# Products of r and v placed in the bank of the product of a, with three operand buffers and two of `ad`

## The chip, the cores and the metric

The kernel runs on one core of one Trainium2 chip. The metric is the device time of one execution in microseconds (us): the kernel before takes 1320.08 us in the median of 3 runs (1316.49 to 1322.68).

A core has five engines that run side by side, each through a list of instructions in a fixed order: TensorE (PE, matrix products, with its weight loads as PEld), VectorE (DVE), ScalarE (ACT), GpSimd (POOL) and SyncE (SP). SP does no arithmetic here; it issues the transfers between memory and the chip (DMAs), one after the other. An instruction whose input isn't ready holds up all that stand behind it on its engine.

## The reference

The input goes through three layers. The first is a recurrence over 768 time steps, for each of 4 x 8 heads with a state of 40 x 40:

```
for t in range(S):
    y[t]  = r[t] @ state
    Sa    = state @ a[t]
    state = state * w[t] - outer(Sa, b[t])
    state = state + outer(v[t], k[t])
```

The other two are gated layers on 3072 tokens of 320 values: `(sigmoid(x @ w_gate) * (x @ w_val)) @ w_out` with 1536 hidden columns, then `h = x @ w_in; (h * sigmoid(1.702 h)) @ w_out` with 2048. The output has 3072 x 320 values.

## The kernel before

**The recurrence in chunks.** The 768 steps are cut into 24 chunks of 32, and each chunk into two halves of two batches each; half h = 0 to 47 belongs to chunk h // 2. Within a chunk the steps are joined to matrix products, and a triangular system takes the place of the step by step update. For a half there are:

- the front (`fronts`, DVE with some help of POOL): running products of w (L699, L705), then `ad` (L728, L740: a scaled, and the decays) and `kb` (L742, L718: b and k scaled). `ad` has four buffers for the first four halves and one for all others.
- the scores (`back`): 16 small products of `ad` and `kb` on PE into the bank pair `s`; DVE multiplies them by masks into `nl` (L795, the triangular system) and `kl` (L802), ACT copies the rest into `kl` (L804). SP stores `nl` as `ldr` (L827), and `ad` and `kl` as `ad_d` and `kl_d` (L809, L812), from where they come back as `ad_l` and `kl_l` when their half's turn comes (L904, L906), some 8 halves later.
- the solve (`solve`): the system of one chunk, or of two after the first four, is loaded (L847), solved by 31 pairs of a multiply and an add (L857, L860), on DVE for the first three chunks and on POOL for the others, stored (L864) and loaded again as `tn` (L874).
- r and v (`preps`, `later`): SP loads r, vt and vn into one of two sets of buffers; PE multiplies r by v (L919) into the same bank pair `s`, and DVE masks that into `vu` (L921).
- the chain (`chain`), which carries the state: PE multiplies `vu` by `kl`, and r by the state `sd`; ACT copies to `xh` (L973); PE multiplies `xh` by a (the "product of a"); ACT copies to `rs` (L1003); PE multiplies `rs` by `tn`, the solved system; DVE's masked copy puts the result into `vu` (L1017); PE multiplies `vu` by `kl` into `po`, from where the next state (L1030, L1037) and the output `yt` (L1052) come.

From half 4 on there is one bank pair `s` for the scores, for r and v, and for the chain's products; the other is given to the first gated layer.

**The gated layers** (`moe1`, `moe2`). The first layer works on pairs of chunks as their outputs come in. Its products (`gv`, `xa`) fill PE between those of the recurrence. The second (`ph`, `y`) begins when the first is done; its weights are decoded on DVE, ACT and POOL once the recurrence has ended.

**The order of the work.** All of this is written as threads, which ask for an engine with a cost, for a buffer (`Slots`) or for an event. A planner (class `Plan`) plays them through, takes for each engine the thread with the lowest key among those that can begin, and writes the instructions in that order. The chip then follows these lists; it doesn't reorder for lateness.

Of the kernel before, what the change touches and what calls it, by code (L numbers as in the profile page):

```python
# [34 lines left out]
C_ID, C_I2, C_UM, C_VM, C_UP, C_SEL, C_END = 0, 128, 168, 200, 234, 306, 338  # L35
# [28 lines left out]
def layout(inp):  # L64
# [13 lines left out]
    def times_on_rows(x):  # L78

        y = x.reshape(2, 2, 2, 2, 2, NCH, C, D)  # L80
        y = np.stack([y[:, :, :, 0], y[:, :, :, 1, ::-1]], axis=3)
        return np.ascontiguousarray(y.transpose(5, 0, 4, 6, 3, 1, 2, 7)).reshape(2 * NCH, 2, C, 8, D)
# [148 lines left out]
def program(ctx: ExitStack, tc: tile.TileContext, abkw, rt, vt, vn, cst, x2, x4, in_r, in_k, in_v, in_w, in_a, in_b, moe_w_gate,  # L231
# [19 lines left out]
    umask, vmask, upred = k[:, C_UM : C_UM + C], k[:, C_VM : C_VM + LT], k[:, C_UP : C_UP + C + D].bitcast(I32)  # L251
# [342 lines left out]
    ring = 2  # L594
# [9 lines left out]
    ads = [wpool.tile([R, I0 + D], F32, tag=f"X{8 + i}", name="ad0") for i in range(4)] + [at.tile([R, I0 + D], F32, name="ad")]  # L604
# [7 lines left out]
    def dims(j):  # L612
        return slice(J * j, J * j + D)
# [7 lines left out]
    def turn_of(h):  # L621

        return h if h < 4 else h % 2
# [29 lines left out]
    e_b, e_vu, e_y = ([Event() for _ in range(NH)] for _ in range(3))  # L653
# [26 lines left out]
    def fronts():  # L680

        thread = plan.current
        for h in range(NH):
# [42 lines left out]
            ad = ads[min(h, START)]  # L726
# [38 lines left out]
    def back(h, kb, ad):  # L765
# [14 lines left out]
        if q == 0:  # L780
            yield nl_slots
            nls[c] = at.tile([128, 2, 8, C], F32, tag="nl", name="nl", bufs=2)
        i = place_of(h)
        yield "PE", 0.55, None, None, plan.WAITS, s_slots[i]
# [7 lines left out]
        if q == 1:  # L792
            yield e_lower_first[c]
# [3 lines left out]
        if q == 0:  # L797
            plan.set(e_lower_first[c])
        else:
            plan.start(scores_out(c), f_key(h) - 0.3, plan.done + plan.LATENCY)  # L800
        yield "DVE", 0.38
        nc.vector.tensor_mul(klv[:, :, :, 0:LT], pt[:, :, :, 0:LT], vmask.unsqueeze(1).unsqueeze(1).broadcast_to([128, 2, 4, LT]))  # L802
# [4 lines left out]
        if h >= START:  # L807
            yield "SP", 0.5
            nc.sync.dma_start(out=st["ad_d"], in_=ad[:, A0:I0])  # L809
            plan.give(ad_slots)  # L810
            yield "SP", 0.5, -9.0
            nc.sync.dma_start(out=st["kl_d"], in_=kl)  # L812
            plan.give(kl_slots)
        plan.set(e_stored[h])

    nls, ldrs = {}, {}
    e_lower_first = [Event() for _ in range(NCH)]

    def scores_out(c):
        cs = group_of[c]  # L820
        if cs not in ldrs:
            ldrs[cs] = drp.tile([2, 2, 8 * len(cs), C, C], F32, tag="ldr", name="ldr", bufs=2)
        yield "SP", 1.2
        nl, u0 = nls.pop(c), 8 * (c - cs[0])
        for i in range(2):
            for o in range(2):
                nc.sync.dma_start(out=ldrs[cs][o, i, u0 : u0 + 8].rearrange("u s t -> s u t"), in_=nl[64 * i : 64 * i + C, o])  # L827
        plan.give(nl_slots)
        if c == cs[-1]:
            plan.start(solve(cs, ldrs.pop(cs), nc.vector if c < DS else nc.gpsimd), s_key(cs), plan.done)  # L830

# [48 lines left out]
    def preps():  # L880

        thread = plan.current
        for h in range(NH):
# [6 lines left out]
            if h >= START:  # L890
                yield e_stored[h]
            yield "SP", 2.5
# [3 lines left out]
            for i in range(2):  # L896
                nc.sync.dma_start(out=vu[64 * i + C : 64 * i + 2 * C, :, C:], in_=vn[h, i])
            t_rv = plan.done
            st = half[h]
            st["vu"] = vu  # L900
            if h >= START:
                yield "SP", 1.0, -9.0
                kl = at.tile([128, KL], F32, tag="kl_l", name="kl_l", bufs=2)
                nc.sync.dma_start(out=kl, in_=st["kl_d"])  # L904
                ad = at.tile([R, I0], F32, tag="ad_l", name="ad_l", bufs=2)
                nc.sync.dma_start(out=ad, in_=st["ad_d"])  # L906
                views(h, ad, kl)
                plan.set(e_stored[h], 0.5)
            plan.set(e_b[h])
            plan.start(later(h, r72, vt_, vu), h - 10, t_rv)  # L910
            yield e_vu[h]

    def later(h, r72, vt_, vu):
        i = place_of(h)
        yield "PE", 0.45, None, None, 0, s_slots[i]
        pv = ss[i][:, :, 0 : 4 * C].rearrange("p o (g n) -> p o g n", g=4)
# [3 lines left out]
        yield "DVE", 0.36  # L920
        nc.vector.tensor_mul(vu[:, :, 0:C].rearrange("p (o g) n -> p o g n", o=2), pv,  # L921
                             vmask[:, 0:C].unsqueeze(1).unsqueeze(1).broadcast_to([128, 2, 4, C]))
# [30 lines left out]
    def chain(hb):  # L953
        thread = plan.current
        for h in range(hb, NH, 2):
# [40 lines left out]
            for gi, g2, o, j, x in HEADS:  # L996
                mm(pr[some(j), o, g2], an[dims(j), gi, 0:LT], xh[o][dims(j), g2], False, True)
# [553 lines left out]
```

## Time and profile before

| | |
|---|---|
| median of 3 runs | 1320.08 us |
| profiled execution | 1315.36 us, span 1313.5 us |
| mean clock of TensorE granted | 0.929 of full |
| PE busy | 1141.2 us (87%) |
| DVE, ACT, POOL busy | 774.8, 451.5, 386.6 us |

The span is the time from the first to the last instruction. Busy time says how much an engine had to do; what decides is where it waited and for whom. The list of waits names the waiting line, the line that released it, the total, the number of times and the longest. PEclk is the share of TensorE's full clock of 2.4 GHz that was granted; it has two levels, full and half. Line numbers L... are those of the kernel before; L578 is the helper that issues all matrix products.

### The profile page before, as it was taken

The page shows a single profiled execution, that of the slowest core. Times are in us where ns is not written, and L with a number is a line of the kernel's source. Part 1 is how long each engine was busy: PE and PEld are TensorE (multiplying, and loading weights), DVE is VectorE, ACT ScalarE, POOL GpSimd, SP SyncE. Part 2 cuts the span into 40 slices and gives each one's busy share as a digit, 9 for nine tenths or more (in the row PEclk, how much of TensorE's full clock was granted, in tenths as well). Part 3 has the DMA queues.
Part 4 walks back from the last instruction along what each step waited for, and adds up shares of the span by engine and source line. Part 5 has one row for each costly group of instructions (what it writes and reads, how often), then busy time and mean ns, then how long its engine had stood idle before and what let it go on. Part 6 is the DMA issues. An engine that isn't in the chain of part 4 may idle for free. (4 is left out here: it accounts for less than half of the span.)

```text
span 1313.5 us, 41904 instructions
## 1 busy us (share of the span) xinstructions
PE 1141.2 (87%) x17601; PEld 1041.9 (79%) x17601; DVE 774.8 (59%) x2074; ACT 451.5 (34%) x1114; POOL 386.6 (29%) x840
## 2 busy tenths in 40 slices
PE   2375648889899999979997999999999899999996
PEld 2265547779798898978887989999889798899995
DVE  7977875445454455545463543337999766556552
ACT  1232322223333232323332323336676243434332
POOL 3212753343435352607070615102432000000000
PEclk9965768679999999989998999999999999999998
DMA  6568565656565657465654555424443432322110
GB/s 176 143 172 235 140 187 143 169 147 168 141 171 123 180 124 192 105 165 142 157 158 110 157 126 130 101 59 137 141 122 94 119 107 56 89 59 79 44 43 23
DMA packets 238340, 168.69 MB, mean 128 GB/s; under 512 B 156800, under 2 KB 204480, under 8 KB 238144
## 3 DMA queue, kind: packets, MB, share of 16 engines
q1 hardware_dynamic: 238144, 165.94, 48.1%
q8 instruction: 140, 2.29, 0.7%
q14 instruction: 56, 0.46, 0.1%
HBM read 123.10 MB, written 42.78 MB: 126 GB/s over the span
## 5 line engine op out<-in xcount | busy, mean ns | idle before, releaser
L578 PE MATMUL gv<-xs,w1i 128*128 128x256 f32 x1728 | 270.3, 298 | 3.1 <-ACT xs L439 3.1
L578 PEld LDWEIGHTS gv<-xs,w1i 128*128 128x128 f32 x1728 | 233.4, 199 | 15.7 <-ACT xs L439 3.5
L857 POOL TENSOR_TENSOR ut<-x,u 128x126 f32<-128x126 f32 (+27 forms) x341 | 139.6, 410 | 186.8 <-DMA x<-in_x_dram 154.2
L578 PE MATMUL y<-w2o,g 128*128 128x320 f32 x1152 | 186.0, 310 | 3.8 <-DVE g L1309 3.3
L578 PE MATMUL xa<-g,w1o 128*128 128x256 f32 x1152 | 186.0, 298 | 3.0 <-DVE g L530 1.4
L578 PEld LDWEIGHTS y<-w2o,g 128*128 128x128 f32 x1152 | 177.2, 189 | 12.4 <-DVE g L1309 3.8
L578 PE MATMUL ph<-xs,w2i 128*128 128x512 f32 x672 | 171.2, 394 | 1.9 <-DVE gg L1301 1.8
L578 PEld LDWEIGHTS xa<-g,w1o 128*128 128x128 f32 x1152 | 156.9, 198 | 13.3 <-DVE g L530 2.3
L860 POOL TENSOR_TENSOR x<-x,ut 128x126 f32<-128x126 f32 (+27 forms) x341 | 143.0, 419 | 26.4
L578 PEld LDWEIGHTS ph<-xs,w2i 128*128 128x128 f32 x672 | 122.5, 188 | 24.5 <-DVE gg L1301 3.3
L523 DVE TENSOR_TENSOR sg<-gv,sg 128x256 f32<-128x256 f32 x144 | 60.4, 419 | 126.2 <-ACT sg L521 126.0
L578 PE MATMUL s<-r,vt 40*64 40x32 f32 x1536 | 64.3, 240 | 66.2 <-DVE vu L1017 55.5
L578 PEld LDWEIGHTS s<-r,vt 40*64 40x64 f32 x1536 | 59.0, 158 | 74.8 <-DVE vu L1017 61.6
L521 ACT ACTIVATE sg<-gv 128x256 f32<-128x256 f32 x144 | 55.2, 383 | 178.5 <-PE gv L578 177.1
L528 ACT CAST g<-sg 128x256 fp32r<-128x256 f32 x144 | 58.6, 407 | 130.0 <-DVE sg L523 114.9
L1301 DVE TENSOR_TENSOR gg<-ph,sg 128x512 f32<-128x512 f32 x96 | 66.0, 687 | 49.6 <-ACT sg L1297 49.6
L1307 ACT CAST g<-gg 128x512 fp32r<-128x512 f32 x96 | 59.5, 620 | 94.8 <-DVE gg L1301 94.6
L1309 DVE TENSOR_TENSOR g<-gg,g 128x512 fp32r<-128x512 f32 x96 | 67.2, 700 | 40.4 <-ACT g L1307 40.4
L728 DVE TENSOR_TENSOR ad<-wx,iw 112x256 f32<-112x256 f32 x45 | 24.3, 540 | 111.0 <-DMA ad_d<-ad 110.9
L578 PE MATMUL s<-ad,kb 40*64 40x80 f32 x1536 | 47.8, 273 | 47.6 <-DVE kb L742 15.9
L1297 ACT ACTIVATE sg<-ph 128x512 f32<-128x512 f32 x96 | 57.2, 596 | 87.9 <-PE ph L578 87.8
L530 DVE TENSOR_TENSOR g<-sg,g 128x256 fp32r<-128x256 f32 x144 | 64.0, 444 | 38.9 <-ACT g L528 38.7
(125 smaller groups left out, 1764.8 us busy)
## 6 DMA issues: line engine op xcount, KB each, us to landing
ab<-in_abkw_dram SPq DMA_DIRECT2D x44, 451.9 KB
kl_d<-kl SPq DMA_DIRECT2D x44, 296.0 KB
kl_l<-kl_d SPq DMA_DIRECT2D x44, 296.0 KB
ad_d<-ad SPq DMA_DIRECT2D x44, 252.0 KB
ad_l<-ad_d SPq DMA_DIRECT2D x44, 252.0 KB
r<-in_rt_dram SPq DMA_DIRECT2D x48, 112.0 KB
vt<-in_vt_dram SPq DMA_DIRECT2D x48, 112.0 KB
u<-ldr SPq DMA_DIRECT2D x20, 256.0 KB
```

The source lines that it names most:

```text
L521: nc.scalar.activation(gg, gv[:, 0, :], AF.Sigmoid)
L523: nc.vector.tensor_mul(gg, gv[:, 1, :], gg)
L528: nc.scalar.copy(out=g4[:, 0], in_=gg)
L530: nc.vector.tensor_sub(out=g4[:, 1], in0=gg, in1=g4[:, 0].bitcast(F32))
L578: nc.tensor.matmul(o, lhsT=w, rhs=x, start=start, stop=stop, skip_group_check=True)
L728: either[on].tensor_mul(dd, wx[:, :, 0:C], iw.broadcast_to([R, 8, C]))
L857: eng.tensor_mul(tv, x[:, :n, s : s + 1].broadcast_to([128, n, m]), u[:, s, s + 1 :].unsqueeze(1).broadcast_to([128, n, m]))
L860: eng.tensor_add(x[:, :n, s + 1 :], x[:, :n, s + 1 :], tv)
L1297: nc.scalar.activation(sg, ph, AF.Sigmoid, scale=1.702)
L1301: nc.vector.tensor_mul(gg, ph, sg)
L1307: nc.scalar.copy(out=g4[:, 0], in_=gg)
L1309: nc.vector.tensor_sub(out=g4[:, 1], in0=gg, in1=g4[:, 0].bitcast(F32))
```

## The change

Each half's product of r and v moves: it is now issued by the chain of the half before, right behind the product of a, into columns 384 to 511 of the same banks, which the chain doesn't use (`r_by_v`, `beside`). Its mask (`masked`) follows the chain's masked copy. r, vt and vu have three sets of buffers instead of two. `ad` has two buffers instead of one. The loads of `kl_l` and `ad_l` (K and B) get a thread of their own (`backs`). `nl` is no longer made: the mask for `kl` keeps both parts, and `ldr` is stored out of `kl`, by half instead of by chunk. v's rows come padded with zeros, in one transfer per half instead of two. The planner books 1.5 us more for the stores of `ad` and `kl`.

```diff
--- before.py
+++ after.py
@@ times_on_rows, the layout of v @@
-        return np.ascontiguousarray(y.transpose(5, 0, 4, 6, 3, 1, 2, 7)).reshape(2 * NCH, 2, C, 8, D)
...
+        z = np.zeros((2 * NCH, 2, 2, C, 8 * D), np.float32)
+        z[:, :, 1] = y.reshape(2 * NCH, 2, C, 8 * D)
+        return z.reshape(2 * NCH, 128, 8, D)
@@ program @@
-    umask, vmask, upred = k[:, C_UM : C_UM + C], k[:, C_VM : C_VM + LT], k[:, C_UP : C_UP + C + D].bitcast(I32)
+    umask, vmask, upred = k[:, C_UM : C_UM + LT], k[:, C_VM : C_VM + C], k[:, C_UP : C_UP + C + D].bitcast(I32)
-    ring = 2
+    ring = 3
-    ads = [wpool.tile([R, I0 + D], F32, tag=f"X{8 + i}", name="ad0") for i in range(4)] + [at.tile([R, I0 + D], F32, name="ad")]
+    ads = [wpool.tile([R, I0 + D], F32, tag=f"X{8 + i}", name="ad0") for i in range(4)] + [at.tile([R, I0 + D], F32, name=f"ad_{i}") for i in range(2)]
-        return h if h < 4 else h % 2
+        return (h if h < 2 else h + 1) if h < 4 else (h - 2) % 3
-    wc_slots, ab_slots, suf_slots, wx_slots, kb_slots, ad_slots, kl_slots = Slots(DEPTH), Slots(2), Slots(1), Slots(1), Slots(2), Slots(1), Slots(1)
+    wc_slots, ab_slots, suf_slots, wx_slots, kb_slots, ad_slots, kl_slots = Slots(DEPTH), Slots(2), Slots(1), Slots(1), Slots(2), Slots(2), Slots(1)
-    nl_slots, u_slots, tn_slots, b_slots, po_slots = Slots(2), Slots(2), Slots(2), Slots(0), Slots(1)
+    u_slots, tn_slots, b_slots, k_slots, po_slots = Slots(2), Slots(2), Slots(0), Slots(2), Slots(1)
-            ad = ads[min(h, START)]
+            ad = ads[h if h < START else START + h % 2]
@@ back @@
-        yield "PE", 0.55, None, None, plan.WAITS, s_slots[i]
+        yield "PE", 0.55, None, None, plan.WAITS if h >= 2 * START else 0, s_slots[i]
...
-        yield "DVE", 0.36, plan.LATENCY
-        nc.vector.tensor_mul(nls[c][:, :, 4 * q : 4 * q + 4], pt[:, :, :, 0:C],
-                             umask.unsqueeze(1).unsqueeze(1).broadcast_to([128, 2, 4, C]))
...
-        yield "DVE", 0.38
-        nc.vector.tensor_mul(klv[:, :, :, 0:LT], pt[:, :, :, 0:LT], vmask.unsqueeze(1).unsqueeze(1).broadcast_to([128, 2, 4, LT]))
+        yield "DVE", 0.4, plan.LATENCY
+        nc.vector.tensor_mul(klv[:, :, :, 0:LT], pt[:, :, :, 0:LT], umask.unsqueeze(1).unsqueeze(1).broadcast_to([128, 2, 4, LT]))
...
-                nc.sync.dma_start(out=ldrs[cs][o, i, u0 : u0 + 8].rearrange("u s t -> s u t"), in_=nl[64 * i : 64 * i + C, o])
-        plan.give(nl_slots)
-        if c == cs[-1]:
+                nc.sync.dma_start(out=ldrs[cs][o, i, u0 : u0 + 4].rearrange("u s t -> s u t"), in_=klv[64 * i : 64 * i + C, o, :, 0:C])
+        stored_of[cs] += 1
+        if stored_of[cs] == 2 * len(cs):
             plan.start(solve(cs, ldrs.pop(cs), nc.vector if c < DS else nc.gpsimd), s_key(cs), plan.done)
+        if h >= START:
+            yield "SP", 0.5, -9.0
+            nc.sync.dma_start(out=st["ad_d"], in_=ad[:, A0:I0])
+            plan.give(ad_slots, 1.5)
+            yield "SP", 0.5, -9.0
+            nc.sync.dma_start(out=st["kl_d"], in_=kl)
+            plan.give(kl_slots, 1.5)
@@ preps: its loads of kl and ad become a thread of their own @@
-            if h >= START:
-                yield e_stored[h]
-            yield "SP", 2.5
+            yield "SP", 1.4
...
-            for i in range(2):
-                nc.sync.dma_start(out=vu[64 * i + C : 64 * i + 2 * C, :, C:], in_=vn[h, i])
+            nc.sync.dma_start(out=vu[:, :, C:], in_=vn[h])
+            plan.start(later(h, r72, vt_, vu), h - 10, plan.done)
+    def backs():
+        for h in range(START, NH):
+            thread.key = h - 1.1
+            yield k_slots
+            yield e_stored[h]
+            yield "SP", 1.0
+            kl = at.tile([128, KL], F32, tag="kl_l", name="kl_l", bufs=2)
+            nc.sync.dma_start(out=kl, in_=st["kl_d"])
+            ad = at.tile([R, I0], F32, tag="ad_l", name="ad_l", bufs=2)
+            nc.sync.dma_start(out=ad, in_=st["ad_d"])
...
     def later(h, r72, vt_, vu):
+        if h > PO2:
+            loaded[h] = (plan.current.ready, r72, vt_, vu)
+            yield e_turn[h]
+            if h not in loaded:
+                return
+            del loaded[h]
...
+    def r_by_v(i, r72, vt_):
+        pv = ss[i][:, :, 512 - 4 * C :].rearrange("p o (g n) -> p o g n", g=4)
         for gi, g2, o, j, x in HEADS:
             mm(pv[times(x), o, g2], vt_[dims(x), C * gi : C * gi + 2 * C], r72[dims(x), gi, 0:C], True, True)
+        return pv
+    def masked(h, vu, pv, i):
+        yield "DVE", 0.42
         nc.vector.tensor_mul(vu[:, :, 0:C].rearrange("p (o g) n -> p o g n", o=2), pv,
...
@@ chain @@
-            yield "PE", 1.0
+            beside = h >= PO2 and h + 1 in loaded and loaded[h + 1][0] + 1.0 < max(ex[0].time, ex[1].time)
+            yield "PE", 1.9 if beside else 1.05
             for gi, g2, o, j, x in HEADS:
                 mm(pr[some(j), o, g2], an[dims(j), gi, 0:LT], xh[o][dims(j), g2], False, True)
+            if beside:
+                _, *rv, vu1 = loaded.pop(h + 1)
+                pv = r_by_v(si, *rv)
...
-            plan.give(s_slots[si])
+            if beside:
+                plan.start(masked(h + 1, vu1, pv, si), h, plan.done)
+            else:
+                plan.give(s_slots[si])
@@ set_up: five sets of r, vt and vu are prepared instead of four @@
```

The planner writes another order on every engine. Three places show it. On PE, in the middle of the recurrence, from one half's product of a (`s<-xh`) to the end of its chain, before; `s<-rs` is the product of the solved system, `s<-r_` that of r and v of the next half, `gv` and `xa` belong to the first gated layer:

```order
L578 MATMUL s<-xh,ad_l 34x72 x16
L578 MATMUL xa<-g_11310,w1o 128x256 x8
L578 MATMUL gv<-xs,w1i 128x256 x6
L578 MATMUL s<-rs,tn_103 34x72 x16
L578 MATMUL gv<-xs,w1i 128x256 x6
L578 MATMUL gv<-xs,w1r 128x256
L578 MATMUL gv<-xz_72,w1r 128x256
L578 MATMUL gv<-xs,w1r 128x256
L578 MATMUL gv<-xz_72,w1r 128x256
L578 MATMUL s<-r_0_86,vt_88 64x32 x16
L578 MATMUL po<-vu_91,kl_l 40x72 x16
```

and in the change:

```order
L580 MATMUL s<-xh,ad_l 34x72 x16
L580 MATMUL s<-r_2_88,vt_91 64x32 x16
L580 MATMUL gv<-xs,w1i 128x256 x6
L580 MATMUL gv<-xs,w1r 128x256
L580 MATMUL gv<-xz_72,w1r 128x256
L580 MATMUL gv<-xs,w1r 128x256
L580 MATMUL gv<-xz_72,w1r 128x256
L580 MATMUL xa<-g_11474,w1o 128x256 x3
L580 MATMUL s<-rs,tn_108 34x72 x16
```

The product of r and v has moved from behind the solved system's to right behind the product of a; in 43 of 48 halves it stands so, before in 2. On SP, around the store of a solved pair of chunks (`xdr`), before:

```order
L864 DMA xdr<-x 1024x1x32 x2
L874 DMA tn_104<-xdr 32x16x32 x4
L893 DMA r_0_86<-in_rt_dram 112x8x32
L894 DMA vt_88<-in_vt_dram 112x256
L897 DMA vu_90<-in_vn_dram 32x8x40 x2
L809 DMA ad_d<-ad 112x576
L812 DMA kl_d<-kl 128x592
```

and in the change:

```order
L852 DMA xdr<-x 1024x1x32 x2
L862 DMA tn_108<-xdr 32x16x32 x4
L950 DMA x1d<-yt 40x4x128 x2
L805 DMA ldr<-kl 32x4x32 x4
L434 DMA xf_9154<-x1d 128x2x256
L436 DMA xf_9154<-x1d 64x256 x2
L811 DMA ad_d<-ad_105 112x576
L814 DMA kl_d<-kl 128x592
```

The stores of `ad` and `kl` stand behind `xdr` and `tn` in both; the stores of `ldr`, now out of `kl`, stand ahead of them too, and the loads of r, vt and vu stand behind. On DVE, ahead of the third solve (its first step is `ut<-x,u 128x31`), before, to row 276 of 2408:

```order
L728 TENSOR_TENSOR ad<-wx,iw 112x256
L733 COPY wc<-wx 112x8
L740 SCALAR_TENSOR_TENSOR ad<-ab,ad 112x8x32
L742 TENSOR_TENSOR kb<-ab,suf 112x8x32
L699 SCALAR_TENSOR_TENSOR wx<-ab,ones 112x264
L705 SCALAR_TENSOR_TENSOR suf<-ab,ones 112x264
L710 TENSOR_SCALAR iw<-wx 112x8
L711 RECIPROCAL iw<-iw 112x8
L1052 TENSOR_TENSOR yt<-po,ad_101 112x2x2x32
L795 TENSOR_TENSOR nl<-s,k 128x2x128
L802 TENSOR_TENSOR kl<-s,k 128x8x34
L857 TENSOR_TENSOR ut<-x,u 128x31
```

and in the change, to row 248 of 2362:

```order
L730 TENSOR_TENSOR ad_106<-wx,iw 112x256
L735 COPY wc<-wx 112x8
L742 SCALAR_TENSOR_TENSOR ad_106<-ab,ad_106 112x8x32
L744 TENSOR_TENSOR kb<-ab,suf 112x8x32
L701 SCALAR_TENSOR_TENSOR wx<-ab,ones 112x264
L707 SCALAR_TENSOR_TENSOR suf<-ab,ones 112x264
L712 TENSOR_SCALAR iw<-wx 112x8
L713 RECIPROCAL iw<-iw 112x8
L277 TENSOR_SCALAR w_1185<-w_955 128x384
L279 SCALAR_TENSOR_TENSOR w_1185<-w_955,w_1185 128x384
L845 TENSOR_TENSOR ut<-x,u 128x31
```

The third solve begins 28 rows earlier, ahead of the third half's masked copy (row 264) instead of behind the fourth's (row 262 before), and its last step stands at row 379 instead of 414.

## Rows read from the trace of the kernel before

**Rows 1.** Busy us (x instructions) of PE, PEld, DVE, ACT, POOL; PEclk, DMA, GB/s.

```profile
100.00:175.00 75.00, 44.33 (x577) 41.13 (x577) 59.99 (x189) 20.52 (x52) 33.55 (x72) 0.68 0.72 195
175.00:300.00 125.00, 96.04 (x2040) 85.36 (x2040) 63.77 (x169) 30.34 (x82) 56.78 (x127) 0.72 0.59 152
300.00:800.00 500.00, 462.85 (x9604) 425.67 (x9606) 250.27 (x658) 154.53 (x409) 199.59 (x461) 0.96 0.59 150
800.00:900.00 100.00, 99.97 (x1966) 92.23 (x1957) 35.16 (x92) 33.60 (x88) 24.88 (x62) 1.00 0.34 86
```

**Rows 2.** Waits, 300 to 800 us: us in total, times, longest.

```profile
PE s L578 <- DVE vu L1017: 31.9, 16, 6.7
...
DVE ad L728 <- DMA ad_d<-ad: 70.7, 22, 9.9
...
SPq L864 <- POOL x L860: 40.1, 7, 8.8
```

**Rows 3.** Waits, 175 to 300 us.

```profile
PE s L578 <- DVE vu L1017: 21.3, 6, 8.8
...
DVE ad L728 <- DMA ad_d<-ad: 32.3, 6, 9.0
```

**Rows 4.** Waits, whole span.

```profile
DVE ad L728 <- DMA ad_d<-ad: 110.9, 32, 9.9
```

**Rows 5.** Timeline of DVE, 349 to 361 us: start, us, engine, line, [idle before].

```profile
349.23 0.43 DVE L530 TENSOR_TENSOR g<-sg,g 128x256 fp32r<-128x256 f32 x1 [1.83 <-ACT g L528]
...
357.52 0.43 DVE L728 TENSOR_TENSOR ad<-wx,iw 112x256 f32<-112x256 f32 x1 [7.87 <-DMA ad_d<-ad]
...
359.59 0.79 DVE L1017 COPY_PREDICATED vu<-k,s 128x576 f32<-128x576 int32 x1
```

**Rows 6.** Timeline of PE, 353 to 363 us.

```profile
353.60 0.88 PE L578 MATMUL gv<-xs,w1i 128*128 128x256 f32 x6
...
360.43 1.81 PE L578 MATMUL s<-r,vt 40*64 40x32 f32 x30 [5.96 <-DVE vu L1017]
```

**Rows 7.** Timeline of SP's issues, 346 to 355 us.

```profile
346.69 1.29 SPq L864 DMA_DIRECT2D xdr<-x  x2
...
352.20 2.13 SPq L874 DMA_DIRECT2D tn<-xdr  x4
...
354.38 0.48 SPq L809 DMA_DIRECT2D ad_d<-ad  x1
```

**Rows 8.** Line L1017: duration min/median/max, first and last start.

```profile
L1017 DVE COPY_PREDICATED vu<-k,s x48: 745/788/819, 64.1 to 885.9; 128x576 f32<-128x576 int32 x48
```

**Rows 9.** Timeline of DVE, 150 to 173 us.

```profile
152.18 0.17 DVE L860 TENSOR_TENSOR x<-x,ut 128x8 f32<-128x8 f32 x1
...
166.84 0.42 DVE L728 TENSOR_TENSOR ad<-wx,iw 112x256 f32<-112x256 f32 x1 [3.69 <-DMA ad_d<-ad]
...
171.81 0.79 DVE L1017 COPY_PREDICATED vu<-k,s 128x576 f32<-128x576 int32 x1
```

**Rows 10.** Timeline of PE and DVE, 476 to 485 us.

```profile
476.59 0.79 DVE L1017 COPY_PREDICATED vu<-k,s 128x576 f32<-128x576 int32 x1
...
477.44 1.06 PE L578 MATMUL s<-r,vt 40*64 40x32 f32 x30
...
481.31 0.77 PE L578 MATMUL s<-ad,kb 40*64 40x80 f32 x32
...
482.82 1.12 PE L578 MATMUL xa<-g,w1o 128*128 128x256 f32 x8
...
483.79 0.64 PE L578 MATMUL gv<-xs,w1i 128*128 128x256 f32 x4
...
484.35 0.71 PE L578 MATMUL s<-vu,kl_l 64*34 64x72 f32 x32
```

**Rows 11.** Waits of PE, 60 to 120 us.

```profile
PE po L578 <- DVE yt L1052: 0.8, 1, 0.8
```

**Rows 12.** Groups by line and form.

```profile
L795 DVE TENSOR_TENSOR nl<-s,k 128x256 f32<-128x256 f32 x48 | 20.2, 420 | 36.2 <-PE s L578 35.8
```

More of the change, by code (lines that the diff above doesn't have):

```diff
@@ L806, in back @@
         plan.set(e_scored[h])
-        if h >= START:
[L808 to L819, printed above, removed]
         cs = group_of[c]
@@ L895, in preps @@
             vu = vus[turn_of(h)]
-            for i in range(2):
-                nc.sync.dma_start(out=vu[64 * i + C : 64 * i + 2 * C, :, C:], in_=vn[h, i])
-            t_rv = plan.done
-            st = half[h]
[L900 to L908, printed above, removed]
@@ L909, in preps @@
-            plan.set(e_b[h])
-            plan.start(later(h, r72, vt_, vu), h - 10, t_rv)
-            yield e_vu[h]
-    def later(h, r72, vt_, vu):
+            nc.sync.dma_start(out=vu[:, :, C:], in_=vn[h])
+            plan.start(later(h, r72, vt_, vu), h - 10, plan.done)
+    def backs():
+        thread = plan.current
+        for h in range(START, NH):
+            thread.key = h - 1.1
+            yield k_slots
+            yield e_stored[h]
+            st = half[h]
+            yield "SP", 1.0
[3 more added lines that the diff above has]
+            nc.sync.dma_start(out=ad, in_=st["ad_d"])
+            views(h, ad, kl)
+            plan.set(e_back[h], 0.5)
@@ L914, in later @@
+    e_turn = [Event() for _ in range(NH)]
+    loaded = {}
+    def later(h, r72, vt_, vu):
+        if h > PO2:
[4 more added lines that the diff above has]
+            del loaded[h]
         i = place_of(h)
-        yield "PE", 0.45, None, None, 0, s_slots[i]
-        pv = ss[i][:, :, 0 : 4 * C].rearrange("p o (g n) -> p o g n", g=4)
+        yield "PE", 0.85, None, None, 0, s_slots[i]
+        yield from masked(h, vu, r_by_v(i, r72, vt_), i)
@@ L923, in later @@
         plan.give(s_slots[i])
         done = plan.done
-        yield e_scored[h]
-        yield e_stored[h]
-        plan.done = max(done, e_scored[h].time, e_stored[h].time)
+        here = (e_stored if h < START else e_back)[h]
+        yield here
+        plan.done = max(done, here.time)
         plan.set(e_vu[h], plan.LATENCY)
@@ L1015, in chain @@
                     plan.give(tn_slots)
-            yield "DVE", 0.68
+            yield "DVE", 0.8
             nc.vector.copy_predicated(out=vuo.rearrange("p (o g) n -> p o g n", o=2), data=pu,
                                       mask=upred.unsqueeze(1).unsqueeze(1).broadcast_to([128, 2, 4, C + D]))
-            plan.give(s_slots[si])
+            if beside:
+                plan.start(masked(h + 1, vu1, pv, si), h, plan.done)
+            else:
+                plan.give(s_slots[si])
             es = [Event(), Event()]
@@ L1063, in results @@
                     plan.give(b_slots)
+                if h >= START:
+                    plan.give(k_slots)
                 passed.append(h)
@@ L1107, in set_up @@
         yield "POOL", 2.0
-        for i in range(2, 4):
+        for i in range(2, 5):
             nc.gpsimd.memset(vus[i], 0.0)
@@ L1111, in set_up @@
         yield e_front[1]
-        for i in range(4):
+        for n in range(START + 1):
             yield "POOL", 1.2
+            i = turn_of(n)
             nc.gpsimd.tensor_copy(out=r72s[i][:, :, C:], in_=i2.unsqueeze(1).broadcast_to([R, 8, D]))
-            if i == 0:
+            if n == 0:
                 yield "POOL", 1.1
                 nc.gpsimd.memset(sd, 0.0)
-            if i % 2:
-                plan.set(e_set[i // 2])
+            if n % 2:
+                plan.set(e_set[n // 2])
+        plan.give(b_slots)
         yield "POOL", 0.5
@@ L1413, in program @@
     plan.start(preps(), 0)
+    plan.start(backs(), 0)
     plan.start(y_outs(), 0)
```

32 lines of the change are left out of this document (14 added, 18 removed).

## The prediction

> **What bounds the kernel now.** I read the kernel by stages first: the busy time of each engine in four stretches [rows 1]. From 800 to 900 us PE is busy 99.97 of 100 us at the full clock (2.4 GHz), and after that the second layer's products run on; nothing that the change touches can shorten that part, it can only begin earlier. From 300 to 800 us PE lacks 500 - 462.85 = 37.2 us, at a mean clock of 0.96, which is full speed with some 8% of the time at the lower level (1.2 GHz): 40 us. From 175 to 300 us it lacks 29.0 us, and the clock is 0.72, so some 56% of 125 us, 70 us, at half speed. So the loss is idle PE ahead of 800 us, and what the clock takes beside it.
>
> Next I ask who keeps PE waiting, in the lists of waits. From 300 to 800 us it is one line: 31.9 of the 37.2 us are PE's wait for L1017, the masked copy of a half's solved values into vu on DVE, in 16 waits [rows 2]; from 175 to 300 us 21.3 of the 29.0 us are the same line, in 6 waits [rows 3]. DVE is only half busy there [rows 1], so L1017 isn't late for want of DVE time. DVE itself waits, at L728, for the store of `ad` to land: 110.9 us over the span [rows 4], 70.7 and 32.3 us in the two stretches [rows 2, 3].
>
> The timelines show one such case from end to end. DVE finishes L530 at 349.66, stands at L728 for 7.87 us until 357.52, and runs L1017, which stands six instructions behind, at 359.59 [rows 5]. PE has nothing left after 354.5 and waits 5.96 us for it [rows 6]. The cause is one queue further: SP holds the stores of `ad` and `kl` behind L864 and L874, the solve's result to memory and back, and issues `ad_d` at 354.38, 7.7 us after L864 [rows 7]; 3.14 us after its issue L728 starts. There is one buffer `ad`, so the next half's front can't write it before the store has read it.
>
> **The change, part by part.** The sum is made against the profiled execution, 1315.4 us (span 1313.5 and 1.9 around it); the median of the runs is 4.7 us above it.
>
> Two buffers of `ad`. L728 of a half now needs the store of the half before last, which in the order stands one whole half earlier; a half takes (885.9 - 171.8) / 43 = 16.6 us [rows 8, 9]. The longest wait at L728 is 9.9 us [rows 2], so these waits go. What is late next? `kl` stays one buffer, and its writer (L802, now L792) waits for `kl_d` and, new, for the four `ldr` stores, which read `kl` too now. All of them still stand behind the solve's two transfers on SP. In the case above the store's landing came 357.52 - 346.69 = 10.8 us after L864. I estimate the new queue to `kl`'s landing from the same rows: L864 to the end of `tn`'s issues as now (352.20 + 2.13 - 346.69, 7.6 us), the four `ldr` stores at 2.13 / 4 = 0.53 us a piece, six other issues in between at some 0.5 us, landing 3.1 us, 15.8 us in all, about the period of a half. So where SP gets to L864 when DVE finishes the earlier `kl`, DVE doesn't wait; where SP stands late, it does, by at most the lateness: L864 waits 40.1 us in 7 cases for the solve, 5.7 us each [rows 2]. Bounds for the new wait: 0, and 5.7 us for each pair of chunks, 40 us where L728 has 70.7. I take the middle, 20 us, that is 28% of what there is, and let 72% of the loss go.
>
> What that is worth from 300 to 800 us: the waits for L1017, 31.9 us, and the work that the clock lost, 40 us at half speed x 0.5 x 0.93 (PE's busy share) = 18.6 us. Together 50 us, of which 72% is 36 us. Bounds: 0 and 50.
>
> From 175 to 300 us: 21.3 us, and 70 x 0.5 x 0.77 = 27 us, together 48 us. Here PE also lacks work, since the first layer's products come out of finished chunks only; the clock can stay low without any wait. I take half, 24 us; bounds 7 (a third of the waits alone) and 40.
>
> r and v moved. Now, after L1017 the bank goes to the product of r and v (477.44), then to the products for `kl` (481.31), and only at 484.35 to the next half [rows 10]: 7.0 us from the end of L1017 (476.59 + 0.79). In 43 of 48 halves the new order has that product right behind the product of a, in the unused columns of the same bank; its mask follows L1017 directly. It costs PE the same 1.06 us; out of the path go one wait of PE for L1017 and one of DVE for PE. Where PE is full (300 us on) that is worth nothing by itself, since the same products fill it; from 175 to 300 us it is part of the half that I took.
> PE has waited in this kernel for a DVE read of other columns of a bank that it was to write: 0.8 us for `yt` [rows 11]. The Trainium skill, PSUM — Partial Sum Buffer, section "PSUM bank collisions raise a hardware error", says that no two engines may be in one bank and strip of partitions at once, disjoint columns included, and that the hardware doesn't arbitrate; so ACT's copy of `rs` has to stand behind the moved product. The trace agrees as far as that one wait goes. By that rule 8 halves from 175 to 300 us lose 8 x 1.06 = 8.5 us again, and the term is 16 instead of 24 and the time 1260 us instead of 1252; from 300 us on PE's other products lie in the gap.
>
> One multiply for `kl` and `nl`. L795 goes, 48 x 0.42 = 20.2 us of DVE [rows 12]. DVE is half busy, so from 175 us on I count nothing; the bank is 0.4 us sooner free.
>
> The start. From 100 to 175 us DVE is busy 60.0 of 75 us [rows 1]: it decodes weights and solves the third chunk, whose last step ends at 152.18; the fifth half's L1017 then comes at 171.81, after a wait of 3.69 us at L728 [rows 9]. In the new order this solve begins at DVE's row 248 instead of 276 and ends at row 379 instead of 414, since the fifth and sixth half's fronts no longer share one `ad`. 35 rows at 59.99 / 189 = 0.32 us are 11 us. Bounds: 0 (the loads from memory decide instead) and 11 + 3.7 = 15.
>
> What it adds. When the fifth half's solved values are copied, 22 fewer of the first layer's products stand ahead on PE (160 against 182); at 0.97 / 8 = 0.12 us each [rows 10] they come later, 3 us. Stores of `ldr` go from 96 to 192 and loads of `vn` from 96 to 48, together 48 issues more at some 0.5 us [rows 7]: 24 us of SP over 700, hidden as long as SP isn't late. `vn` moves 160 KB a half instead of 80; the 16 DMA engines are 0.59 busy [rows 1], and I count nothing. The third buffers of r, v and vu and the own thread for K and B only move loads forward; they cover 16 us of lateness more, which I have not counted.
>
> Sum: 36 + 24 + 11 - 3 = 68 us. 1315.4 - 68 = 1247.4, and 4.7 for the median: **1252 us**.
>
> **Rivals.**
> A, the single `kl` takes `ad`'s place. For it: the same queue, and more stores ahead of it. Against it: `kl` is written later in a half than `ad`. A third of the first two terms is left: 20 + 11 - 3 = 28 us, 1292 us. It decides where `kl_d` lands over one half after the earlier `kl` was written.
> B, everything goes: 50 + 40 + 15 - 3 = 102 us, 1218 us. For it: three operand buffers absorb what is late. Against it: the solve's lateness on SP stays.
> C, no change: the real end is the solve chain, and all waits follow it. Against it: POOL, which solves, is 40% busy from 300 to 800 us [rows 1]. 1320 us.
> D, slower: SP's one queue becomes the path. A half has 16.5 issues (counted in the new order) of some 0.55 us [rows 7], 9.1 us, and its share of waits for the solve, 5.7 / 4 = 1.4 us; the stores of `ldr`, `ad` and `kl` wait in line with loads that the chain needs. It decides from the point where the waits of the stores for their data pass 6 us a half; then the halves follow SP. At 1 us a half over today's 16.6 that is 43 us, less 8 at the start: 1355 us. Against it: 9.1 and 1.4 leave 6 us of each half.
>
> **How the numbers follow.** Forecast 0.60, A 0.20, B 0.09, C 0.04, D 0.07. The forecast's own range is 1228 to 1278; to hold 8 in 10 with A's 1292 and half of B inside, 1217 to 1303. Within 0.5% (6.6 us, about what a measurement of this kernel can tell from no change) lie C and the rim of A, 0.05; slower is D, 0.07; faster the rest, 0.88.
>
> **What would show it.** L728's wait for `ad_d` (110.9 us) near zero, and PE's wait for L1017's successor at 15 to 20 us from 300 to 800 us in place of 31.9. A wait of DVE at L792 for `kl_d` or `ldr` of up to 20 us there: more than 45 is A. The fifth masked copy at some 160 us instead of 171.8. A mean clock over 0.98 from 300 to 800 us and over 0.8 before it. PE busy 99% after attention ends, as now. If the clock from 175 to 300 us stays at 0.7, the second term is wrong; if SP is late everywhere and the period of a half is over 16.6 us, it is D.

## The result, and the profile after

The changed kernel takes 1302.78 us in the median of 4 runs (1300.09 to 1305.18), the kernel before, run beside it, 1318.28 us (1315.15 to 1322.68). The ratio is 0.9879, with a 95% interval of 0.9841 to 0.9918. So it is faster by some 16 us, where 68 were forecast. Some times below come from other chips and runs, so kernels are compared by their ratio to the kernel before, and a difference of ratios is turned into us with 1318.

The four stretches of [rows 1], in the changed kernel (columns as there):

```profile
100.00:175.00 75.00, 52.38 (x904) 47.81 (x904) 67.90 (x197) 27.52 (x75) 42.09 (x85) 0.73 0.63 179
175.00:300.00 125.00, 95.28 (x2118) 86.28 (x2118) 58.45 (x155) 34.01 (x92) 57.17 (x134) 0.81 0.67 162
300.00:800.00 500.00, 467.85 (x9993) 432.45 (x9994) 247.32 (x642) 157.96 (x415) 211.80 (x505) 0.96 0.67 160
800.00:900.00 100.00, 94.97 (x1467) 89.47 (x1466) 46.10 (x133) 41.30 (x118) 14.71 (x29) 0.97 0.33 85
```

From 300 to 800 us PE lacks 32.2 us, before 37.2, at the same clock of 0.96; from 175 to 300 us it lacks 29.7, before 29.0, at a clock of 0.81 for 0.72. From 800 to 900 us, where it lacked nothing, it now lacks 5.0. The waits from 300 to 800 us answer to [rows 2]:

```profile
ACT xs L441 <- DMA xf<-x1d: 42.3, 7, 8.1
POOL ad L730 <- DMA ad_d<-ad: 40.8, 3, 14.7
...
PE s L580 <- ACT rs L1013: 34.0, 8, 7.2
...
DVE ad L730 <- DMA ad_d<-ad: 29.4, 13, 9.6
...
PE po L580 <- DVE vu L1030: 1.7, 3, 1.1
```

PE's wait for the masked copy (L1017 before, L1030 now; 31.9 us) is all but gone, at 1.7 us, and 34.0 us of waiting for `rs` stand in its place. The wait for `ad_d` isn't gone: 70.2 us on DVE and POOL together, for 70.7. From 175 to 300 us, where [rows 3] had 21.3 us for the masked copy:

```profile
DVE ad L730 <- DMA ad_d<-ad: 27.1, 4, 10.9
...
PE gv L580 <- ACT xs L441: 9.4, 1, 9.4
...
PE s L580 <- DVE vu L925: 8.4, 3, 3.5
```

L925 is the mask of r and v's product into `vu` (L921 before).

One case of the new wait. SP's issues behind the end of a solve on POOL (start, us, engine, line):

```profile
351.02 1.41 SPq L852 DMA_DIRECT2D xdr<-x  x2
354.56 2.65 SPq L862 DMA_DIRECT2D tn<-xdr  x4
357.32 0.78 SPq L950 DMA_DIRECT2D x1d<-yt  x2
358.14 1.78 SPq L805 DMA_DIRECT2D ldr<-kl  x4
360.03 0.38 SPq L434 DMA_DIRECT2D xf<-x1d  x1
360.45 1.13 SPq L436 DMA_DIRECT2D xf<-x1d  x2
361.63 0.58 SPq L811 DMA_DIRECT2D ad_d<-ad  x1
```

ACT in the same stretch:

```profile
355.65 0.42 ACT L530 CAST g<-sg 128x256 fp32r<-128x256 f32 x1
362.91 0.62 ACT L441 CAST xs<-xf 128x512 fp32r<-128x512 f32 x1 [6.83 <-DMA xf<-x1d]
...
363.86 0.40 ACT L446 CAST xh<-xf 64x256 fp32r<-64x256 f32 x1
364.28 0.64 ACT L1013 COPY rs<-s 98x576 f32<-98x576 f32 x1
```

And PE:

```profile
360.10 0.52 PE L580 MATMUL xa<-g,w1o 128*128 128x256 f32 x3
364.97 0.82 PE L580 MATMUL s<-rs,tn 34*34 34x72 f32 x32 [4.36 <-ACT rs L1013]
```

It is the picture of [rows 5 to 7] with another victim. The solve ends, SP sends `xdr` and `tn`, and behind them wait the store of the output, the stores `ldr` and the load `xf`, the input of the first gated layer. ACT stands at the cast of it (L441) for 6.83 us, and behind the cast, in ACT's list, is `rs`, which the chain needs. In 9 of the 12 pairs of chunks the new order has the cast between `xh` and `rs`; before it stood there in 2.

The masked copies, by the line's first and last start [rows 8] and the fifth [rows 9]:

```profile
L1030 DVE COPY_PREDICATED vu<-k,s x48: 759/821/831, 70.1 to 864.8; 128x576 f32<-128x576 int32 x48
```

```profile
160.88 0.82 DVE L1030 COPY_PREDICATED vu<-k,s 128x576 f32<-128x576 int32 x1
```

The recurrence ends 21.1 us sooner, the span 14.1. The chain's lead has to be counted with the first layer's products that stand ahead of it in PE's list, at the 0.12 us each of the prediction:

| masked copy | before | after | sooner | products ahead, before / after | sooner, in work |
|---|---|---|---|---|---|
| 5th | 171.81 | 160.88 | 10.9 | 182 / 160 | 8.3 |
| 8th | 224.47 | 205.97 | 18.5 | 272 / 272 | 18.5 |
| 9th | 238.54 | 237.89 | 0.7 | 272 / 294 | 3.3 |
| 13th | 307.88 | 302.90 | 5.0 | 440 / 526 | 15.3 |
| 41st | 791.79 | 758.88 | 32.9 | 2542 / 2446 | 21.4 |
| last | 885.93 | 864.83 | 21.1 | 2992 / 2940 | 14.9 |

By stage the last column gives 8 us at the start, 7 from the 5th to the 13th copy, 6 from there to the 41st, and 6.5 given back at the end. The windows agree within some 2 us: busy time times clock is 8 us more than before from 175 to 300 us, 5 more from 300 to 800 and 8 less from 800 to 900.

### The profile page after: what moved, and what is told of

It reads as the page before. It is cut to its first block, busy times and chain, and to the rows that moved or that the text cites. A ratio compares the mean times of both kernels' runs of the same rounds, so it can differ in the third digit from the quotient of the medians.

```text
span 1299.4 us, 42036 instructions
## 1 busy us (share of the span) xinstructions
PE 1130.5 (87%) x17601; PEld 1035.8 (80%) x17601; DVE 757.9 (58%) x2017; ACT 451.8 (35%) x1114; POOL 387.1 (30%) x854
## 5 line engine op out<-in xcount | busy, mean ns | idle before, releaser
L845 POOL TENSOR_TENSOR ut<-x,u 128x126 f32<-128x126 f32 (+27 forms) x341 | 136.5, 400 | 175.0 <-DMA x<-in_x_dram 148.8
L580 PE MATMUL xa<-g,w1o 128*128 128x256 f32 x1152 | 182.9, 296 | 3.2 <-DVE x L483 1.7
L580 PE MATMUL s<-rs,tn 34*34 34x72 f32 x1536 | 41.5, 252 | 48.1 <-ACT rs L1013 40.0
L580 PE MATMUL gv<-xs,w1r 128*128 128x256 f32 x288 | 82.4, 304 | 0.0
L580 PE MATMUL gv<-xz,w1r 128*128 128x256 f32 x288 | 77.8, 288 | 0.0
L580 PE MATMUL s<-ad,kb 40*64 40x80 f32 x1536 | 43.7, 261 | 38.4 <-DVE kb L720 11.6
```

Source lines behind the costliest of these rows:

```text
L580: nc.tensor.matmul(o, lhsT=w, rhs=x, start=start, stop=stop, skip_group_check=True)
L845: eng.tensor_mul(tv, x[:, :n, s : s + 1].broadcast_to([128, n, m]), u[:, s, s + 1 :].unsqueeze(1).broadcast_to([128, n, m]))
```

## The experiments

Theory 1: the wait moved from DVE to ACT, through the place of one cast. Theory 2: the solved system itself is late, since the scores lead the chain's masked copy by 6 halves and not 7. Theory 3: the turns in the bank set the period. Theory 4: all of it hangs on the solve, which ends later than the planner's order allows for.

**e1**, the cast booked later:

```diff
                 nc.sync.dma_start(out=xf[64 * o : 64 * o + 64, 2, :], in_=x1d[256:320, at_])
+            if p >= 2 and o:
+                plan.current.ready += 6.0
```

> The changed kernel, with one booking of the planner altered: from the third pair of chunks on, the cast of the first layer's input (xs, ACT, L441) is booked 6 us later, so that on ACT it stands behind the copy rs in all ten pairs, where in the changed kernel it stands between xh and rs in nine. Every transfer and product stays. Theory 1 (ACT's queue: the cast waits for xf, whose load stands on SP behind the solve, and rs waits behind the cast): PE's waits for rs from 300 to 800 us, 34.0 us in 8, fall under 8 us, and the time falls by these and some clock, 25 to 45 us, to 1258 to 1278 us. Theory 2 (the solved system itself is late, because the fronts lead the chain by 6 halves instead of 7): the same 25 to 34 us come back as a wait of PE for tn, and the time stays within 6 us of 1303.

Measured: 1277.11 us, ratio 0.9685 (0.9649 to 0.9721), 26 us less than the changed kernel. Waits from 300 to 800 us:

```profile
DVE ad L732 <- DMA ad_d<-ad: 68.7, 21, 8.0
...
PE po L582 <- DVE vu L1032: 20.7, 9, 5.1
```

No wait for `rs` and none for `tn` is left there, and theory 2 falls for this stretch. The booking that moves the cast is worth 26 us. That the cast's place alone holds them isn't shown: the planner also moved other instructions on every engine, the first write of `ad` of six halves from POOL to DVE among them. Of the 20.4 us between the two profiled executions, 13 lie between the 13th and the 41st masked copy and 7 behind the 41st, with the first layer's products counted as in the table. The wait for `ad_d` shows again, in PE's wait for the masked copy.

**e2**, the solve of a pair booked 5 us later:

```diff
         nc.sync.dma_start(out=x, in_=x2 if nr == 2 else x4)
+        if len(cs) == 2:
+            plan.current.ready += 5.0
```

> The changed kernel, with the planner told that the solve of two chunks begins 5 us later than it thought (the trace shows it late by about that, SP waiting 45.4 us in 11 cases for POOL at L852). On SP the loads of xf then stand ahead of the store xdr, and on ACT the cast stands behind rs from the fifth pair on. The chain's lead of fronts stays 6. Theory 1: SP's wait for POOL falls under 25 us, PE's waits for rs under 12 us from 300 to 800 us, DVE's and POOL's waits for ad_d shrink, time 1260 to 1280 us. Theory 2: the solve is what is late, a longer booking moves only the order, PE waits for tn instead, time 1297 to 1310 us.

Measured: 1305.62 us, 0.9917 (0.9881 to 0.9952). SP's wait for POOL fell to 16.6 us and the waits for `rs` from 300 to 800 us to 1.2, as theory 1 has it, and no gain came of it. One stall is seen: PE's list now has products of the third pair too early,

```profile
313.11 0.80 PE L580 MATMUL gv<-xs,w1i 128*128 128x256 f32 x2 [11.69 <-ACT xs L441]
```

and `tn` is waited for 3.9 us only, so theory 2's time is met without its reason.

**e3**, the third solve keyed later:

```diff
-        return 2 * cs[0] - SK if cs[0] else -1
+        return 3.0 if cs[0] == 2 else 2 * cs[0] - SK if cs[0] else -1
```

> The changed kernel, with the third solve (DVE) keyed later, so that the fronts of the next halves come ahead of it, as they did in the kernel before: the fronts lead the chain by 7 halves again from the fifth half on, instead of 5 and 6. The cast xs still stands between xh and rs on ACT in most pairs. Theory 1: the start gives back its 11 us, the gap of 31.9 us ahead of the ninth half's masked copy closes to under 20 us, and PE's waits for rs from 300 to 800 us stay at 20 to 34 us, since the order on ACT is the same: 1290 to 1305 us. Theory 2: those waits go too (under 10 us), as the solved system comes a half earlier against the chain: 1262 to 1280 us.

Measured: 1319.22 us, 1.0016 (0.9991 to 1.0042). Neither: the fifth masked copy came at 180.82 us, 20 us later; the gap ahead of the ninth closed from 31.9 to 18.1; the waits for `rs` went from 300 us on, though the cast still stands between `xh` and `rs` in 10 of the 12 pairs: it waits 2.7 us at most there. But DVE's wait for `ad_d` is 109.5 us over the span, and with it, from 300 to 800 us,

```profile
PE po L580 <- DVE vu L1030: 28.4, 7, 7.1
```

A lead of 7 halves didn't help: the waiting went back to DVE.

**e4**, the second buffer alone, in the kernel before:

```diff
...
-    ... ad_slots, kl_slots = ... Slots(1), Slots(1)
+    ... ad_slots, kl_slots = ... Slots(2), Slots(1)
-            ad = ads[min(h, START)]
+            ad = ads[h if h < START else START + h % 2]
```

> The kernel before, with two buffers of ad and nothing else of the change. The prediction's main term alone: DVE's wait for ad_d at L728 (110.9 us) falls under 30 us, and with it PE's waits for the masked copy (31.9 us from 300 to 800 us) to under 12 us, worth 40 to 60 us: 1258 to 1278 us. Theory 1 says the gain hangs on where the cast xs stands on ACT, which in this kernel is ahead of rs in 5 of 12 pairs: half of the waits come back as waits for rs, 1280 to 1295 us. The rival that the end is the solve: 1313 to 1325 us.

Measured: 1340.95 us, 1.017 (1.0137 to 1.0204): slower by 22 us, which no theory had. Over the span:

```profile
DVE ad L728 <- DMA ad_d<-ad: 114.1, 36, 9.6
```

The wait is as long as with one buffer [rows 4]. The fronts run further ahead: the first write of `ad` comes 10 halves ahead of the chain's masked copy, with one buffer 8; the scores 8 ahead, with one buffer 7. And the write of a half again stands right behind the store it needs: from that store's issue to the write it is 3.3 us in the median, with one buffer 3.5, in the changed kernel 3.0. SP's wait for the solve can't account for it: from 300 to 800 us that is 14.0 us in 4 cases, where [rows 2] have 40.1, while DVE's wait there is 75.1 for 70.7. Of the loss, 21 us are there by the 13th masked copy (329.22 for 307.88 us), the first 11 at the fifth (183.10).

**e5**, e1 with the buffer of `ad` booked free later; **e13** the same with that write kept on DVE:

```diff
-            plan.give(ad_slots, 1.5)
+            plan.give(ad_slots, 9.0 if h >= 12 else 1.5)
```

```diff
-            on = yield "EITHER", 0.45, 0.12, None, 0.8
+            on = yield ("DVE" if h >= 12 else "EITHER"), 0.45, 0.12, None, 0.8
```

> The kernel of e1 (cast behind rs), and from half 12 on the planner books the buffer of ad free 9 us after its store instead of 1.5, so that it no longer places the next write of ad right behind the landing. Theory (the second buffer gave no slack: the planner spent it on running the fronts one half further ahead, and the write of a half still stands 2.6 to 5 us behind the issue of the store it needs, as with one buffer): DVE's wait for ad_d, 92.7 us in e1, falls under 35 us, and PE's waits for the masked copy, 20.7 us from 300 to 800 us, under 8 us; with the clock 12 to 22 us, so 1255 to 1265 us. Rival (the write comes late because the front itself is late, or another wait stands in its place): waits on DVE fall but the time stays within 6 us of 1277.

> The kernel of e5 (cast behind rs, the buffer of ad booked free 9 us after its store from half 12 on), and from half 12 on the first write of ad is kept on DVE. In e5 the planner put it on POOL in some halves, amid the steps of the solve that ran late (580.66 us), and DVE, ACT and PE waited in turn. Theory: that is what e5 lost, so the waits of PE for xh (15.1 us in 5) and yt (10.6 in 5) fall under 8 us together, DVE's wait for ad_d stays under 35 us: 1258 to 1275 us. Rival (a later front takes its lead from the solve, wherever its write stands): 1288 to 1302 us, as e5's 1295.

Measured: 1295.41 us (0.9826, 0.9784 to 0.9867) and 1292.97 us (0.9793, 0.9747 to 0.9838). In e5 the write stands 10.5 us behind the issue of its store in the median, in e13 11.0, and the wait for `ad_d` is all but gone: in e5 none is seen from 300 to 800 us, and over the span there is

```profile
DVE ad L732 <- DMA ad_d<-ad: 9.4, 2, 6.2
```

Other waits stand in its place, from 300 to 800 us:

```profile
PE s L582 <- ACT xh L979: 15.1, 5, 4.3
...
PE po L582 <- DVE yt L1070: 10.6, 5, 4.3
```

Slower than e1 by 19 and 14 us, and the place on POOL isn't the reason. What it is stays open: the rest of the order moved too.

**e6**, e1 with one buffer of `ad`; **e7**, e1 with r and v not beside (the edit of e7):

```diff
-            beside = h >= PO2 and h + 1 in loaded and ...
+            beside = False and h + 1 in loaded and ...
```

> The kernel of e1 with one buffer of ad, as before the change; r and v beside the product of a, the three operand buffers, the one multiply and the own thread for K and B stay. The prediction's reckoning: the waits for ad_d and what hangs on them come back, 40 to 60 us, 1317 to 1337 us. Theory (the second buffer only shifts the fronts): within 10 us of 1277, and the wait for ad_d at 80 to 130 us as in e1 (92.7).

> The kernel of e1 with the product of r and v never beside the product of a: it asks for the bank by itself, behind the chain, as before the change. All else of the change stays. The prediction held this part to be worth little from 300 us on, where PE is full (within 8 us of 1277). Theory 3 (the bank pair is what sets the period of a half: scores, r and v, and the chain take turns in it, and beside takes one turn out): each half is 1 to 1.5 us longer, 43 to 60 us in all, 1305 to 1340 us, with the period of four halves back at 68 to 70 us.

Measured: 1307.91 us (0.9925, 0.9901 to 0.995), so the second buffer is worth 32 us beside the rest; and 1315.05 us (0.999, 0.9967 to 1.0014), so the moved product is worth 40. The two don't add up: e1 as a whole is 42 us below the kernel before, and no run leaves out both. In e7 four halves take 67.3 us on average (13th to 45th copy), in e1 62.5, and

```profile
PE s L582 <- DVE vu L1032: 30.0, 10, 7.4
```

is the wait of [rows 2] come back, with PE idle 38.4 us from 300 to 800 us (25.1 in e1) and the clock at 0.92 (0.97), which is 13 us of idle time and some 23 of clock (0.05 x 462). Theory 3's time is met, its 68 to 70 us for four halves just missed.

**e8**, the kernel before with e1's booking:

> The kernel before, with only the cast of the first layer's input booked 6 us later, as in e1; it stands behind rs in all pairs from the third on, where before it stood ahead of rs in two. Theory 1 in its plain form (the changed kernel's lost gain is this place on ACT, which the kernel before hardly had): no change, 1308 to 1322 us. Rival (the cast ahead of the chain's copies costs the kernel before as much): 1280 to 1295 us, and the gain of e1 isn't the change's.

Measured: 1316.25 us, 0.9992 (0.9963 to 1.002). The booking gains nothing in the kernel before; e1's 26 us are the changed kernel's own loss. One thing stays unexplained: in the profiled execution, 5.5 us under the median, PE's wait for the masked copy from 300 to 800 us is 16.0 us instead of 31.9, and the median shows no gain.

**e9, e10, e12**, the solve of a pair cut to 16 of 31 steps in the changed kernel, the one before and e1, with the order of PE, DVE, ACT and SP kept (the add of each step is left out likewise):

```diff
-            eng.tensor_mul(tv, x[:, :n, s : s + 1].broadcast_to([128, n, m]),
+            if len(cs) == 1 or s < 16:
+              eng.tensor_mul(tv, x[:, :n, s : s + 1].broadcast_to([128, n, m]),
...
```

> The changed kernel with its order kept on PE, DVE, ACT and SP, word for word; only the last 15 of the 31 steps of each solve of two chunks are left out on POOL (so the solved system isn't the reference's). The solve then ends some 15 us sooner than now. Theory 4 (the one cause is that the solve of a pair ends 5 to 6 us later than the planner's order allows for, and SP, which waits for it, holds what stands behind: the stores of ad, or xf; which engine pays depends on the order): SP's wait for POOL at L852, 45.4 us, falls under 8, PE's waits for rs, 34.0 us, under 4, and the time to 1245 to 1265 us. Rival (the cast would wait for its input anyway, since x1d is stored just ahead): the waits for rs stay over 20 us and the time over 1285.

> The kernel before with its order kept on PE, DVE, ACT and SP; as in e9 only the last 15 of 31 steps of each solve of two chunks are left out on POOL (so the solved system isn't the reference's). Theory 4: SP's wait for POOL at L864, 61.3 us, falls under 12; DVE's wait for ad_d, 110.9 us, at least halves; PE's wait for the masked copy, 53.2 us from 175 to 800 us, falls under 20; the time is 1262 to 1285 us, the same gain as the shorter solve gives in the changed kernel within 15 us. The prediction's reckoning of all that hangs on ad (50 and 48 us) would give 1217 to 1240. Rival (ad's one buffer holds the front whatever SP does): within 10 us of 1316.

> The kernel of e1 with its order, and the last 15 of 31 steps of each solve of two chunks left out on POOL (so the solved system isn't the reference's). Theory 4: what e1 still loses to the solve from 175 us on is the wait for the masked copy (20.7 us) and part of the gap at the ninth half: 1240 to 1262 us, and DVE's wait for ad_d (92.7 us) under 45. If e1 already took all that the solve's lateness costs: 1270 to 1280.

Measured: 1271.15 us (0.9639, 0.9585 to 0.9693), 1284.24 us (0.9749, 0.9703 to 0.9794) and 1259.38 us (0.9581, 0.9531 to 0.963). The shorter solve is worth 32 us in the changed kernel, 33 in the one before and 14 in e1: the change took none of that cost away, e1's booking more than half. Against e9, that booking is worth 8 us only, within the intervals, where with the whole solve it was 26. POOL's other work comes sooner too when the solve is short, and no run here keeps the two apart. In e10, from 300 to 800 us:

```profile
DVE ad L728 <- DMA ad_d<-ad: 54.9, 23, 5.1
...
PE s L578 <- DVE vu L1019: 8.6, 9, 2.1
```

Against [rows 2] the wait for `ad_d` fell only from 70.7 to 54.9 us, but its longest from 9.9 to 5.1, and PE's wait from 31.9 to 8.6. So most of DVE's waiting is followed by no wait of PE; the long ones are. Beside the case of [rows 5, 6] two more of the kernel before show it, DVE first and PE behind:

```profile
564.86 0.43 DVE L728 TENSOR_TENSOR ad<-wx,iw 112x256 f32<-112x256 f32 x1 [8.28 <-DMA ad_d<-ad]
...
704.82 0.42 DVE L728 TENSOR_TENSOR ad<-wx,iw 112x256 f32<-112x256 f32 x1 [9.88 <-DMA ad_d<-ad]
```

```profile
567.78 1.81 PE L578 MATMUL s<-r,vt 40*64 40x32 f32 x30 [6.71 <-DVE vu L1017]
...
708.93 1.81 PE L578 MATMUL s<-r,vt 40*64 40x32 f32 x30 [6.62 <-DVE vu L1017]
```

With the 5.96 us of [rows 6] these are 19.3 of the 31.9 us. In e9 PE still waits 16.8 us for `rs`, as the cast waits for `xf` even then. On SP, ahead of `xf`, the issue of `tn` waits until `xdr` has landed (300 to 800 us):

```profile
SPq L864 <- DMA xdr<-x: 31.3, 8, 4.6
```

Theory 4 holds for about half of the 34 us.

**e11**, both bookings:

> The changed kernel with both bookings: the cast of the first layer's input 6 us later from the third pair on (e1), and the solve of a pair 5 us later (e2). Theory 4: with the solve booked as late as it is, neither ad_d nor xf waits behind it, and e2's stall at 313 us (PE for xs, 11.7 us) goes as the cast is booked later: 1252 to 1272 us, below e1. Rival (e2's loss is in the booking itself: more of the first layer's products come ahead of the chain, and each half is longer): 1280 to 1305 us.

Measured: 1295.22 us, 0.9834 (0.9779 to 0.9888). Its rival's time came: booking the solve as late as it is gives a worse order than e1's.

**e14, e15**, e12 with r and v not beside, and with one `ad`:

> The kernel of e12 (cast behind rs, the last 15 of 31 steps of each solve of two chunks left out, so the solved system isn't the reference's), with the product of r and v not beside the product of a. The prediction's reckoning: worth nothing from 300 us on, some 5 to 10 us before, so 1259 to 1270 us. Theory 3 (a turn in the bank for each half): 25 to 45 us are lost even when the solve is never late, 1284 to 1304 us.

> The kernel of e12 (cast behind rs, the last 15 of 31 steps of each solve of two chunks left out, so the solved system isn't the reference's), with one buffer of ad. If the second buffer is worth only what the solve's lateness costs (the prediction's reason for it): within 6 us of 1259. If it lets the fronts run further ahead and that lead has a worth of its own: 1270 to 1290 us, as with the whole solve, where one buffer cost 31 us (e6 against e1).

Measured: 1289.47 us (0.9788, 0.9738 to 0.9839) and 1268.92 us (0.9615, 0.9567 to 0.9663). With a solve that isn't late the moved product still gives 27 us, and the second buffer 5, within the intervals. In e15, from 300 to 800 us,

```profile
DVE ad L732 <- DMA ad_d<-ad: 51.4, 16, 7.1
...
PE po L582 <- DVE vu L1034: 9.0, 7, 2.5
```

DVE waits 51.4 us for the one buffer, and PE 9.0 us for the masked copy.

The fastest kernel with the whole solve is e1: 1277.11 us, 3.15% below the kernel before.

## Why the prediction was wrong

**Two buffers of `ad`: "so these waits go". This step failed.** It held the order fixed and asked how far away the store of the half before last stands. But the planner starts a front as soon as a buffer is free, so a second buffer is spent on running further ahead (the first write of `ad` 8 halves ahead in e1, 7 with one buffer in e6; 10 in e4, 8 in the kernel before), and the write stands as close behind its store as ever (3.0 us in the median for 3.5). The waits were 110.9 us and are 91.3 (50.5 on DVE, 40.8 on POOL); alone the buffer made the kernel slower (e4). Its worth showed only with the rest of the change and a late solve (32 us, e6; 5 without, e15). The Trainium skill, Trainium Kernel Development and Optimization, section "Best Practices", advises double buffering to overlap transfers with compute; e4 is a case where that alone cost 1.7%.

**"72% of the loss".** The waits for the masked copy did go, but I asked only what is late next on DVE, and named `kl`, at which DVE never waited for a transfer. Late next was ACT: `rs` behind the cast. The Trainium skill, PSUM — Partial Sum Buffer, section "Engine vs sequencer instructions", says that ACT, DVE and POOL work through their queues strictly in order. The trace agrees: `rs` begins 0.02 us after the cast's last part (363.86 + 0.40), although PE ended the two products ahead of it at 358.88. The term of 36 us came out at 6. Of the missing 30, e1 gives back some 13 in this stretch; in the rest PE waits for the masked copy again (20.7 us in e1). It could be seen before: the new order of ACT lists the cast ahead of `rs`, and SP's order `xf` behind the solve.

**r and v: "worth nothing by itself" where PE is full.** Wrong by 27 to 40 us (e14, e7), most of it from 300 to 800 us: there busy time times clock is 30 and 36 us less without the move. PE was not full there; it lacked 37.2 us. The wait of 31.9 us was a wait of this very product: [rows 6] name `s<-r,vt` as what stood still. I read its releaser and gave the whole of it to `ad`. Behind the move the next to wait for the same copy is `po<-vu` (20.7 us in e1, 30.0 for `s<-r,vt` in e7). The cost that the prediction weighed is there: ACT's wait for PE ahead of `rs` rose from 45.7 us in 39 times to 77.6 in 34, that is 1.2 to 2.3 us each, by the 1.06 us of the product; it is small against what the move gives.

**175 to 300 us.** 24 us were taken, 7 came. The waits for the masked copy went there too, but PE stood 9.4 us for `xs` and 8.4 for L925, and the clock rose to 0.81 only. The sum of the stage hides a step back: the 8th masked copy came 18.5 us sooner, the 9th 0.7. In between lie PE's wait for `xs`,

```profile
221.72 1.95 PE L580 MATMUL gv<-xs,w1i 128*128 128x256 f32 x6 [9.42 <-ACT xs L441]
```

and the first solve of two chunks on POOL, whose `xdr` SP sends at 224.26 us, before at 211.3.

**The start: right.** The fifth masked copy at 160.88 us (some 160 forecast), 8.3 us in work for 11 - 3.

**The end: not foreseen.** PE waits 4.5 us for `rs` after 800 us and has 52 more products of the first layer left: 6.5 us given back.

**The rivals.** The measured 1302.78 us lies at the far rim of the range, 1217 to 1303. A's 1292 us is nearest, and it is of A's kind: a wait took the place of the one removed, though not at `kl`. D, a slower kernel through SP, didn't come: SP has 48 issues more, and from the 13th to the 41st copy four halves take 65.1 us, before 69.1. Of the signs named, L728's wait near zero and a clock over 0.98 from 300 to 800 us (it is 0.96) failed at once; a clock over 0.8 ahead of it came, just (0.81).

What stays open: why the orders of e2, e5, e11 and e13, which take away the waits they aim at, give less than e1; and how much of e4's loss is the third solve alone. Each of the bookings, and e4, e6, e7, e14 and e15 too, moves hundreds of instructions, and no run among them holds the rest still; only e9, e10 and e12 keep an order. The third buffers of r, v and `vu`, the one multiply and the thread for K and B were not tried alone.

## What to carry to other kernels

A buffer added for a producer that runs ahead until its buffers are full can move the producer ahead and leave its write as close behind the store as before; ask where the write will stand in the new order, not only how many buffers there are. Distance alone isn't a gain either: e5 and e13 had it, and were slower than e1. Before counting a wait as gain, read which instruction waits, and what else stands behind the same late transfer in every engine's list: the late solve on SP's queue stopped DVE before the change and ACT behind it. The sum of an engine's waits says little; its longest ones, and whether the engine that sets the time waits then, say more.

## What was not expected of the hardware

The granted clock of the first 100 us differed between kernels with the same order there: 0.72 in e1 and 0.94 in e12, while PE was busy 40.3 and 38.8 us and the fifth masked copy came at 162.78 and 159.81 us. In e13 it was 0.74, with the copy at 161.42, and in the changed kernel 0.94, with the copy at 160.88. In a stretch where PE mostly waits, the clock said little about the time here.
